# Five transposed weights for the backward pass: transposed by TensorE and kept in DRAM, or loaded by transposing DMAs

## The chip, the cores and the metric

The kernel runs on one core of a Trainium2 chip. The metric is the device time of one execution in microseconds (us). In the profile PE is TensorE (matmuls; PEld are its weight loads), DVE is VectorE, ACT is ScalarE, POOL is GpSimd and SP is the engine that issues all the DMAs of this kernel, on one queue.

## The reference

The reference computes a four-layer network and all its gradients. Layers 0 and 2 are the same linear-attention block, layers 1 and 3 the same gated block, each on a layernorm of the residual stream x, with shared weights:

```python
def _A_ref(x, wqkv, wo):          # H = 32 heads of 16
    q, k, v = (x @ wqkv) split into heads
    pq, pk = phi(q), phi(k)       # phi(t) = where(t > 0, t + 1, exp(t)) + 1e-6
    kv = einsum("bhsd,bhse->bhde", pk, v); z = einsum("bhsd->bhd", pk)
    o = einsum("bhqd,bhde->bhqe", pq, kv) / (einsum("bhqd,bhd->bhq", pq, z)[..., None] + 1e-6)
    return merge_heads(o) @ wo

def _B_ref(x, w_gate, w_up, w_down):
    h = sigmoid(x @ w_gate) * (x @ w_up)
    return h @ w_down

x = x + _A_ref(_layernorm(x), A_wqkv, A_wo)
x = x + _B_ref(_layernorm(x), B_w_gate, B_w_up, B_w_down)
...                                # the same two lines once more
_out, _vjp = jax.vjp(_f, A_x, A_wqkv, A_wo, B_w_gate, B_w_up, B_w_down)
return (_out, *_vjp(grad_out))
```

The sequence has 2048 rows (S), the width D is 512, the gated width F is 1376, everything in bfloat16. wqkv is 512 x 1536, wo 512 x 512, w_gate and w_up 512 x 1376, w_down 1376 x 512.

## The kernel before

The sequence is cut into 16 tiles of 128 rows (NST = 16, index `st`). The forward pass goes through the layers in order. `kq_fwd` makes an attention layer's k and q for all tiles; `ab_fwd` then goes once over the tiles and does, for each, the rest of the attention layer (`attn_y`, line 809 on TensorE) and the whole gated layer behind it (`gu`, line 864; `transposes`, line 878; `finish`, line 890). What the backward pass needs is stored in DRAM (tensors `sv_...`), since SBUF does not hold it.

The backward pass is `b_bwd_p1(3)`, the attention backward of layer 2 (`A2.first`, `A2.second`), `b_bwd_p1(1)`, and the attention backward of layer 0 (`A0.first`, `A0.second`). The weight gradients are sums over all tiles; generators (`p2_gen`, lines 1330 and 1342) hand out their matmuls in units, which are put between the matmuls of the attention passes, and what is left is done at the end. `p2_gen` loads one set of operands ahead (`p_set`).

The order of TensorE, DVE, ACT and POOL is the order in which the program states the work (`tc.manual_schedule(engines=EM)`) in most stages; in `second` and on SP's queue a scheduler places the instructions. Each engine takes its instructions in order, and SP issues DMAs in order; a DMA shares one of eight completion semaphores with the DMA eight places earlier and is issued once that one has landed.

The backward pass multiplies by transposed weights. They are made in the forward pass. A `Fill` object holds 16 groups for `ab_fwd` of layer 1 (`wT_groups_a`: wqkv and wo) and 34 groups for that of layer 3 (`wT_groups_b`: w_down, w_up, w_gate). A group is three or four 128 x 128 TensorE transposes into one PSUM tile `wT_ps` (lines 369, 395, 412) and one eviction on DVE or ACT (lines 341, 343). Six groups of each layer are put at the start of the stage (four in `A.tail`, one `A.extra`, one in tile 0); the others are spread over the later tiles:

```python
def share(self, st):
    return (self.n - self.done) // (NST - st)
```

In layer 1 this gives no group in tiles 1 to 5 and one in each tile from 6 on; in layer 3 one group in tiles 1 and 2, and two in each tile from 3 on. The groups of layer 1 are stored to DRAM (`wqkvT_d`, `woT_d`). Those of layer 3 are evicted right into `wdT`, `wuT` and `wgT`, where `b_bwd_p1(3)` uses them, and stored to DRAM too (`wdT_d`, `wuT_d`, `wgT_d`).

The backward weights live in a pool `wb` with three buffers: `w_c` (wdT, later MT and X of the attention), `w_a` (wuT, later wqkvT) and `w_b` (wgT, later woT and GT). So they are loaded anew for each layer: `load_a_weights` at the start of `A2.first` and `A0.first` (lines 247 to 252), `load_b_weights` ahead of `b_bwd_p1(1)` (lines 235 to 239). In `ABwd.first` the loads of the tiles' `pqn` (line 1463) and `phq_ld` (line 1031) stand behind them on SP's queue; DVE's step for a tile needs `phq_ld` (line 1453).

F is 10 chunks of 128 and one of 96 (`FLAST`). In `b_bwd_p1` the last chunk of `ddT` is transposed and multiplied with 96 rows, and evicted by a copy of its own (lines 1085 and 1087).

## Time and profile before

| what | value |
|---|---|
| time, median of 3 runs | 1215.07 us (1214.5 to 1217.31) |
| the profiled execution: time, span | 1216.08 us, 1214.3 us |
| granted TensorE clock, mean | 0.999 |
| PE busy | 1185.4 us, 98% of the span, 8646 matmuls |
| DVE, ACT, POOL busy | 726.9, 599.9, 259.1 us |
| DMA | 256.08 MB, 66.0% of 16 engines over the span |
| weight transposes on TensorE (`wT_ps`) | 196, in layer 1 from 72.6 to 214.0 us, in layer 3 from 277.6 to 428.0 us |
| plain reload of wdT, wuT, wgT (layer 1) | 1376, 1408, 1408 KB; 10.3, 6.5, 7.7 us to landing |
| plain loads of wqkvT and woT (layers 2 and 0) | 1536 and 512 KB; 9.0 and 8.2 us to landing, median of 2 |

The span is from the first to the last instruction; the execution's time has some us around it. [...] "Idle before, releaser" names what an engine waited for just before an instruction. The stages lie in the trace like this: layer 0's k and q to 72 us, layer 1's `ab_fwd` to 225, layer 2's k and q to 277, layer 3's `ab_fwd` to 433, `b_bwd_p1(3)` to 570, the attention backward of layer 2 to 707, held-back weight-gradient matmuls and `b_bwd_p1(1)` to 931, the attention backward of layer 0 to 1070, and the last weight gradients.

### The profile page before, as it was taken

The numbers are of one execution on the slowest core, as the hardware profiler recorded it, in microseconds if no ns is written. First come the engines' busy times: TensorE is split into PE (matmuls) and PEld (weight loads), VectorE is DVE, ScalarE is ACT, GpSimd is POOL, SyncE is SP. The second block draws the span as 40 slices with busy tenths as digits, with TensorE's granted clock in tenths as the row PEclk, the third lists the DMA queues.
The fourth block names the chain that finished last, engine by engine and source line by source line (L and its number), as shares of the span: only waits on it lengthen the run. The fifth ranks groups of instructions, "written<-read, shape, count | busy, mean of one in ns | idle before, by whom it ended". The sixth has DMA issues, their size and how long they took to land. (4 is left out here: it accounts for less than half of the span.)

```text
span 1214.3 us, 22436 instructions
## 1 busy us (share of the span) xinstructions
PE 1185.4 (98%) x8646; PEld 716.8 (59%) x8646; DVE 726.9 (60%) x1410; ACT 599.9 (49%) x1105; POOL 259.1 (21%) x467
## 2 busy tenths in 40 slices
PE   7989999998999999999999999999999999999998
PEld 4445555454555555555665566765556755577777
DVE  6778887777777556565786730056666966742221
ACT  5677776647767644445537631145445527620001
POOL 4236675204665410000110010000100101100000
PEclk9999999999999999999999999999999999999999
DMA  7934545435546696967866469687667766569974
GB/s 231 311 118 144 197 157 181 172 122 176 185 150 231 232 279 184 312 187 236 229 188 203 147 222 322 206 281 218 213 194 246 206 219 180 170 172 351 293 234 135
DMA packets 266203, 256.08 MB, mean 211 GB/s; under 512 B 43248, under 2 KB 250992, under 8 KB 261232
## 3 DMA queue, kind: packets, MB, share of 16 engines
q1 hardware_dynamic: 266096, 254.65, 66.0%
q8 instruction: 67, 1.10, 0.4%
q14 instruction: 40, 0.33, 0.1%
HBM read 135.69 MB, written 118.92 MB: 210 GB/s over the span
## 5 line engine op out<-in xcount | busy, mean ns | idle before, releaser
L1342 PE MATMUL p_ps<-p_set,p_a 128*128 128x256 bf16 (+1 forms) x1792 | 186.8, 263 | 0.0
L1016 DVE TENSOR_TENSOR dd<-dhh_ps,ssd 128x512 bf16<-128x512 f32 x144 | 82.5, 629 | 149.0 <-PE dhh_ps L1008 142.1
L1342 PEld LDWEIGHTS <-p_a 128*128 128x128 bf16 x1792 | 160.3, 98 | 18.7
L1085 ACT COPY ddT<-T_ps 128x1024 bf16<-128x1024 bf16 (+1 forms) x96 | 82.9, 868 | 126.5 <-PE T_ps L1083 126.5
L870 POOL TENSOR_TENSOR ssd_t<-hh_t,oms 128x512 bf16<-128x512 bf16 (+1 forms) x96 | 101.6, 1064 | 53.6 <-ACT out_t L212 40.9
L1117 PEld LDWEIGHTS <-ddT 128*128 128x128 bf16 (+1 forms) x704 | 66.4, 98 | 68.6
L864 PEld LDWEIGHTS <-hT 128*128 128x128 bf16 x768 | 71.2, 98 | 57.8 <-DVE hT L341 1.5
L982 POOL TENSOR_SCALAR ab<-c 128x2 f32<-128x2 f32 x64 | 12.5, 196 | 433.2 <-DVE junk L979 416.4
L864 PE MATMUL g_ps<-wg,hT 128*128 128x512 bf16 (+1 forms) x384 | 90.0, 357 | 1.1 <-DVE hT L341 1.1
L1321 DVE TENSOR_TENSOR dw_stg<-p_ps,dw_stg 128x512 bf16<-128x512 f32 (+2 forms) x43 | 28.4, 659 | 103.3 <-PE p_ps L1342 80.8
L864 PE MATMUL u_ps<-wu,hT 128*128 128x512 bf16 (+1 forms) x384 | 90.0, 357 | 0.0
L869 DVE TENSOR_TENSOR hh_t<-u_ps,ssd_t 128x512 bf16<-128x512 f32 (+1 forms) x96 | 61.0, 636 | 46.9 <-PE u_ps L864 26.7
L1117 PE MATMUL dh_ps<-wgT,ddT 128*128 128x512 bf16 (+1 forms) x352 | 86.2, 379 | 0.0
L1008 PE MATMUL dhh_ps<-wdT,gT 128*128 128x512 bf16 x372 | 82.5, 357 | 0.5 <-DVE dd L1016 0.5
L890 PE MATMUL y_ps<-wd,hhT 128*128 128x512 bf16 (+1 forms) x352 | 81.3, 379 | 0.6 <-DVE x L892 0.6
L1117 PE MATMUL dh_ps<-wuT,ddT 128*128 128x512 bf16 (+1 forms) x352 | 81.3, 379 | 0.0
L1330 PE MATMUL p_ps<-p_a,p_set 128*128 128x512 bf16 (+1 forms) x352 | 80.4, 379 | 0.0
L866 ACT ACTIVATE ssd_t<-g_ps 128x512 bf16<-128x512 f32 (+1 forms) x96 | 53.2, 554 | 31.7 <-PE g_ps L864 31.4
L974 ACT ACTIVATE t_sb<-dh_ps,rstd_all 128x512 f32<-128x512 f32 x64 | 44.0, 688 | 36.6 <-issue 18.4
L979 DVE SCALAR_TENSOR_TENSOR junk<-t_sb,h_ld 128x512 bf16<-128x512 f32 x60 | 41.2, 687 | 34.8 <-ACT t_sb L974 34.8
L1323 ACT CAST dw_stg<-p_ps 128x512 bf16<-128x512 f32 (+2 forms) x43 | 24.2, 563 | 72.1 <-PE p_ps L1342 51.8
L1330 PEld LDWEIGHTS <-p_set 128*128 128x128 bf16 (+1 forms) x352 | 34.4, 100 | 35.5
(236 smaller groups left out, 2184.9 us busy)
## 6 DMA issues: line engine op xcount, KB each, us to landing
p_set<-sv_hdd SPq DMA_DIRECT2D x30, 1024.0 KB, 6.4
sv_ssd<-ssd_t SPq DMA_DIRECT2D x32, 688.0 KB, 3.5
ssd<-sv_ssd SPq DMA_DIRECT2D x24, 688.0 KB, 5.0
sv_hdd<-dd SPq DMA_DIRECT2D x48, 320.0 KB, 3.3
sv_hdd<-hh_t SPq DMA_DIRECT2D x32, 320.0 KB, 2.6
p_set<-sv_dqk SPq DMA_DIRECT2D x8, 1024.0 KB, 5.4
h_ld<-sv_h SPq DMA_DIRECT2D x30, 256.0 KB, 4.5
p_a<-sv_h SPq DMA_DIRECT2D x12, 512.0 KB, 6.5
```

Of the source, the lines that this page charges most:

```text
L864: nc.tensor.matmul(ps[:, 0:w], lhsT=hT[:, kc, :], rhs=w_sb[:, kc, c0:c0 + w], start=(kc == 0), stop=(kc == NDC - 1))
L866: nc.scalar.activation(ssd_t[:, 0, c0:c0 + w], g_ps[:, 0:w], ACT.Sigmoid)
L869: nc.vector.tensor_tensor(hh_t[:, c0:c0 + w], u_ps[:, 0:w], ssd_t[:, 0, c0:c0 + w], ALU.mult)
L870: nc.gpsimd.tensor_tensor(ssd_t[:, 1, c0:c0 + w], hh_t[:, c0:c0 + w], oms[:, 0:w], ALU.mult)
L890: nc.tensor.matmul(y_ps[:], lhsT=T["hhT"][0:r, fc, :], rhs=k.wd[0:r, fc, :], start=(fc == 0), stop=(fc == NFC - 1))
L974: k.nc.scalar.activation(self.t[:], dh_ps, ACT.Identity, scale=rstd_col, accum_out=self.c12[:, 0:1])
L1008: k.nc.tensor.matmul(ps[:, 0:w], lhsT=gT[:, jc, :], rhs=k.wdT[:, jc, c0:c0 + w], start=(jc == 0), stop=(jc == NDC - 1))
L1016: k.nc.vector.tensor_tensor(dd[:, a, c0:c0 + w], ps[:, 0:w], ssd[:, a, c0:c0 + w], ALU.mult)
L1085: nc.scalar.copy(ddT[:, :, fcs[0]:fcs[0] + nfull, :], tps[:, :, 0:nfull, :])
L1117: nc.tensor.matmul(T["dh"][:], lhsT=T["ddT"][0:r, a, fc, :], rhs=(k.wuT, k.wgT)[a][0:r, fc, :], start=(i == 0), stop=(i == 2 * NFC - 1))
L1330: nc.tensor.matmul(ps[0:r, :], lhsT=set_t[:, st, j * P:j * P + r], rhs=g_all[:, st, :], start=(st == 0), stop=(st == NST - 1))
L1342: nc.tensor.matmul(ps[:, icl * w:(icl + 1) * w], lhsT=h_all[:, st, ic * P:(ic + 1) * P], rhs=set_t[:, st, 0:w], start=(st == 0), stop=(st ...
```

## The change

The five weights are no longer transposed by TensorE. Each buffer of the backward weights is loaded by transposing DMAs (`dma_start_transpose`) straight from the kernel's inputs, at every place where it was made or reloaded. `wT_groups_a`, `wT_groups_b` and the DRAM tensors of the transposed weights are gone, and both `Fill` objects are empty. `load_b_weights` is now called for layer 3 too, from `out_cb` of tile 1. A transposing DMA of w_up and w_gate moves chunks of 128 columns, so the last chunk is loaded from columns 1248 to 1375: its first 32 rows repeat columns that chunk 9 has, and a POOL memset zeroes them after the load. `b_bwd_p1` therefore treats the last chunk as a full one: 128 rows in the transposes and matmuls, and one eviction instead of two.

```diff
+    def load_b_weights():
+        wb = k.wb
+        k.wdT = wb.tile([P, NDC, F], BF16, name="wdT", tag="w_c")
+        nc.sync.dma_start_transpose(out=k.wdT[:], in_=B_w_down)
+        k.wuT = wb.tile([P, NFC, D], BF16, name="wuT", tag="w_a")
+        k.wgT = wb.tile([P, NFC, D], BF16, name="wgT", tag="w_b")
+        for t_sb, w_d in ((k.wuT, B_w_up), (k.wgT, B_w_gate)):
+            nc.sync.dma_start_transpose(out=t_sb[:, 0:NFC - 1, :], in_=w_d[:, 0:(NFC - 1) * P])
+            nc.sync.dma_start_transpose(out=t_sb[:, NFC - 1:NFC, :], in_=w_d[:, F - P:F])
+            nc.gpsimd.memset(t_sb[0:P - FLAST, NFC - 1, :], 0.0)
...
-            with tc.tile_pool(name="wt_stage", bufs=2, reuse_waits="tile") as wt_stage:
-                fill = Fill(wT_groups_a(k, wt_stage))
-                A.tail(fill)
-                ab_fwd(k, A, lns[1], fill, nxt=lns[2])
+            fill = Fill([])
+            A.tail(fill)
+            ab_fwd(k, A, lns[1], fill, nxt=lns[2])
...
             def out_cb(st):
+                if st == 1:
+                    k.load_b_weights()
...
-            fill = Fill(wT_groups_b(k, wb))
+            fill = Fill([])
...
-        def load_b_weights():
-            k.wdT = wb.tile([P, NDC, F], BF16, name="wdT", tag="w_c")
-            nc.sync.dma_start(out=k.wdT[:], in_=k.wT["wdT"].rearrange("(c p) f -> p c f", p=P))
-            k.wuT = wb.tile([P, NFC, D], BF16, name="wuT", tag="w_a")
-            k.wgT = wb.tile([P, NFC, D], BF16, name="wgT", tag="w_b")
-            for t_sb, t_d in ((k.wuT, k.wT["wuT"]), (k.wgT, k.wT["wgT"])):
-                nc.sync.dma_start(out=t_sb[:], in_=t_d.rearrange("(c p) j -> p c j", p=P))
...
-            nc.sync.dma_start(out=k.wqkvT[:], in_=k.wT["wqkvT"].rearrange("(c p) j -> p c j", p=P))
+            nc.sync.dma_start_transpose(out=k.wqkvT[:], in_=A_wqkv)
...
-            nc.sync.dma_start(out=k.woT, in_=k.wT["woT"].rearrange("(c p) j -> p c j", p=P))
+            nc.sync.dma_start_transpose(out=k.woT, in_=A_wo)
...
-                    r = fc_rows(fc)
-                    nc.tensor.transpose(tps[0:r, a, i, :], dd[:, a, fc * P:fc * P + r], k.ident[:])
-            if nfull > 0:
-                nc.scalar.copy(ddT[:, :, fcs[0]:fcs[0] + nfull, :], tps[:, :, 0:nfull, :])
-            if nfull < len(fcs):
-                nc.scalar.copy(ddT[0:FLAST, :, NFC - 1, :], tps[0:FLAST, :, nfull, :])
+                    c0 = min(fc * P, F - P)
+                    nc.tensor.transpose(tps[:, a, i, :], dd[:, a, c0:c0 + P], k.ident[:])
+            nc.scalar.copy(ddT[:, :, fcs[0]:fcs[0] + len(fcs), :], tps[:, :, 0:len(fcs), :])
...
-                r = fc_rows(fc)
-                nc.tensor.matmul(T["dh"][:], lhsT=T["ddT"][0:r, a, fc, :], rhs=(k.wuT, k.wgT)[a][0:r, fc, :],
+                nc.tensor.matmul(T["dh"][:], lhsT=T["ddT"][:, a, fc, :], rhs=(k.wuT, k.wgT)[a][:, fc, :],
```

On SP's queue the scheduler puts wdT's transposing DMA of layer 3 behind the last store of pk of layer 2, wuT's first one behind the store of X, and the other three behind the store of MT; they come ahead of the stores of layer 3's first tile. In `A2.first` the order on the queue stays: wqkvT, woT, three loads of pqn, then phq. In `A0.first` the first load of phq, which stood ahead of the three loads of pqn, now stands behind them. On POOL the two memsets of layer 3 stand together, behind the layernorm scalars of tile 3.

More of the change, by code (lines that the diff above doesn't have):

```diff
@@ L120 @@
         k.sv[l] = d
-    k.wT = dict(
-        wqkvT=dram.tile([3 * D, D], BF16, name="wqkvT_d"),
-        woT=dram.tile([D, D], BF16, name="woT_d"),
-        wgT=dram.tile([NFC * P, D], BF16, name="wgT_d"),
-        wuT=dram.tile([NFC * P, D], BF16, name="wuT_d"),
-        wdT=dram.tile([D, F], BF16, name="wdT_d"),
-    )
     k.dwp = dict(
@@ L133 @@
     )
+    def load_b_weights():
[8 more added lines that the diff above has]
+            nc.gpsimd.memset(t_sb[0:P - FLAST, NFC - 1, :], 0.0)
+    k.load_b_weights = load_b_weights
     k.rstd = [keep.tile([P, NST], F32, name=f"rstd_all{l}") for l in range(4)]
@@ L194 @@
             hctx.close()
-            wb = bctx.enter_context(tc.tile_pool(name="wbwd", bufs=1, side="right", reuse_waits="tile"))
+            wb = k.wb = bctx.enter_context(tc.tile_pool(name="wbwd", bufs=1, side="right", reuse_waits="tile"))
             ocur = {}
@@ L248, in load_a_weights @@
             k.wqkvT = wb.tile([P, 3 * NDC, D], BF16, name="wqkvT", tag="w_a")
-            nc.sync.dma_start(out=k.wqkvT[:], in_=k.wT["wqkvT"].rearrange("(c p) j -> p c j", p=P))
+            nc.sync.dma_start_transpose(out=k.wqkvT[:], in_=A_wqkv)
             woT_GT = wb.tile([P, 2, NDC, D], BF16, name="woT_GT", tag="w_b")
             k.woT, k.GT = woT_GT[:, 0, :, :], woT_GT[:, 1, :, :]
-            nc.sync.dma_start(out=k.woT, in_=k.wT["woT"].rearrange("(c p) j -> p c j", p=P))
-        k.load_b_weights, k.load_a_weights, k.load_MT = load_b_weights, load_a_weights, load_MT
+            nc.sync.dma_start_transpose(out=k.woT, in_=A_wo)
+        k.load_a_weights, k.load_MT = load_a_weights, load_MT
         R = P2Res(k,
@@ L353, in dram_batch @@
     return ap2d[batch_rows(b, nb), :].rearrange("(n p) d -> p n d", p=P)
-def wT_groups_a(k, stage):
-    nc = k.nc
-    groups = []
-    for w_sb, wT_d, C in ((k.wqkv, k.wT["wqkvT"], 3 * D), (k.wo, k.wT["woT"], D)):
-        for cc0 in range(0, C // P, 4):
-            holder = {}
-            for j in range(4):
-                def g(bank, w_sb=w_sb, wT_d=wT_d, cc0=cc0, j=j, holder=holder):
-                    if j == 0:
-                        holder["t"] = stage.tile([P, 4, D], BF16, name="wt_st")
-                    cc = cc0 + j
-                    ps = ps_tile(k, bank, [P, 8, P], BF16, "wT_ps")
-                    for rc in range(NDC):
-                        nc.tensor.transpose(ps[:, rc, :], w_sb[:, rc, cc * P:(cc + 1) * P], k.ident[:])
-                    def ev(eng):
-                        evac_copy(k, holder["t"][:, j, :], ps[:, 0:NDC, :].rearrange("p a b -> p (a b)"), eng)
-                        if j == 3:
-                            nc.sync.dma_start(
-                                out=wT_d[cc0 * P:(cc0 + 4) * P, :].rearrange("(n p) d -> p n d", p=P),
-                                in_=holder["t"][:])
-                    return ev
-                groups.append(g)
-    return groups
@@ L382, in wT_groups_b @@
-def wT_groups_b(k, wb):
-    nc = k.nc
-    groups = []
-    k.wdT = wb.tile([P, NDC, F], BF16, name="wdT", tag="w_c")
-    k.wuT = wb.tile([P, NFC, D], BF16, name="wuT", tag="w_a")
-    k.wgT = wb.tile([P, NFC, D], BF16, name="wgT", tag="w_b")
-    for cc in range(NDC):
-        for fs in range(3):
-            def g(bank, cc=cc, fs=fs):
-                fcs = fchunks_of_slice(fs)
-                ps = ps_tile(k, bank, [P, 8, P], BF16, "wT_ps")
-                for i, fc in enumerate(fcs):
-                    r = fc_rows(fc)
-                    nc.tensor.transpose(ps[:, i, 0:r], k.wd[0:r, fc, cc * P:(cc + 1) * P], k.ident[0:r, 0:r])
-                c0, w = FSL[fs]
-                def ev(eng):
-                    evac_copy(k, k.wdT[:, cc, c0:c0 + w], ps[:].rearrange("p a b -> p (a b)")[:, 0:w], eng)
-                    if cc == NDC - 1 and fs == 2:
-                        nc.sync.dma_start(out=k.wT["wdT"].rearrange("(c p) f -> p c f", p=P), in_=k.wdT[:])
-                return ev
-            groups.append(g)
-    for w_sb, wT_sb, wT_d in ((k.wu, k.wuT, k.wT["wuT"]), (k.wg, k.wgT, k.wT["wgT"])):
-        for cc in range(NFC):
-            def g(bank, w_sb=w_sb, wT_sb=wT_sb, wT_d=wT_d, cc=cc):
-                r = fc_rows(cc)
-                if cc == 0:
-                    nc.gpsimd.memset(wT_sb[FLAST:P, NFC - 1, :], 0.0)
-                ps = ps_tile(k, bank, [P, 8, P], BF16, "wT_ps")
-                for rc in range(NDC):
-                    nc.tensor.transpose(ps[0:r, rc, :], w_sb[:, rc, cc * P:cc * P + r], k.ident[:])
-                def ev(eng):
-                    evac_copy(k, wT_sb[0:r, cc, :], ps[0:r, 0:NDC, :].rearrange("p a b -> p (a b)"), eng)
-                    if cc == NFC - 1:
-                        nc.sync.dma_start(out=wT_d.rearrange("(c p) j -> p c j", p=P), in_=wT_sb[:])
-                return ev
-            groups.append(g)
-    return groups
@@ L1077, in transposes @@
             fcs = fchunks_of_slice(fs)
-            nfull = len([fc for fc in fcs if fc_rows(fc) == P])
             tps = ps_tile(k, "t", [P, 2, 4, P], BF16, "T_ps")
@@ L1115, in dh_mm @@
                 a, fc = divmod(i, NFC)
-                r = fc_rows(fc)
-                nc.tensor.matmul(T["dh"][:], lhsT=T["ddT"][0:r, a, fc, :], rhs=(k.wuT, k.wgT)[a][0:r, fc, :],
+                nc.tensor.matmul(T["dh"][:], lhsT=T["ddT"][:, a, fc, :], rhs=(k.wuT, k.wgT)[a][:, fc, :],
                                  start=(i == 0), stop=(i == 2 * NFC - 1))
```

## The prediction

> **What bounds the kernel now.** I read the page first, then TensorE's waits, its timeline, the DMA share by stretches, and last DVE's, SP's and POOL's timelines where the loaded weights are used. The chain of waits reaches back only to 1067 us, where the edit no longer acts, so the stages decide. In fences with columns "start us, us", x4 counts instructions.

> ```profile
> PE 1185.4 (98%) x8646; PEld 716.8 (59%) x8646; DVE 726.9 (60%) x1410; ACT 599.9 (49%) x1105; POOL 259.1 (21%) x467
> ```

> TensorE is busy 98% of the span, and its named waits sum to 24 us, most at the starts of stages or in the two attention backward passes. So removed TensorE work counts, at its price in the row of instructions, not at its shown duration. That price is in TensorE's timeline of the first GLU forward (layer 1):

> ```profile
> 114.01 1.03 PE L809 MATMUL y_ps<-M_sb,pqnT 128*128 128x512 bf16 x4
> ...
> 123.25 1.03 PE L809 MATMUL y_ps<-M_sb,pqnT 128*128 128x512 bf16 x4
> ...
> 132.23 1.03 PE L809 MATMUL y_ps<-M_sb,pqnT 128*128 128x512 bf16 x4
> 133.09 0.39 PE L369 MATMUL wT_ps<-ident,wqkv 128*128 128x128 bf16 x4
> 133.31 1.03 PE L864 MATMUL g_ps<-wg,hT 128*128 128x512 bf16 x4
> ...
> 141.45 1.03 PE L809 MATMUL y_ps<-M_sb,pqnT 128*128 128x512 bf16 x4
> ...
> 150.66 1.03 PE L809 MATMUL y_ps<-M_sb,pqnT 128*128 128x512 bf16 x4
> ```

> A group of four weight transposes moves the next matmul by 133.31 - 133.09 = 0.22 us (busy time says 0.39). L809 comes once per row tile: with a group the period is 9.21 to 9.22 us, without one 9.24 and 8.98 in turn, mean 9.11. So removing a group in layer 1 is worth 0.11, not 0.22: without it every second tile waits for DVE's pqnstage. The same in layer 3, with one and with two groups per tile:

> ```profile
> 291.80 1.03 PE L809 MATMUL y_ps<-M_sb,pqnT 128*128 128x512 bf16 x4
> ...
> 300.97 1.03 PE L809 MATMUL y_ps<-M_sb,pqnT 128*128 128x512 bf16 x4
> ...
> 338.42 1.03 PE L809 MATMUL y_ps<-M_sb,pqnT 128*128 128x512 bf16 x4
> ...
> 347.82 1.03 PE L809 MATMUL y_ps<-M_sb,pqnT 128*128 128x512 bf16 x4
> ```

> 9.17 with one group, 9.40 with two: here the second costs its full 0.23.

> **What goes.** 196 transposes in 50 groups. In each layer six groups stand at the start of the stage; behind them TensorE waits for hstage, hT or pqnstage anyway (0.95, 0.56 and 1.8 us in layer 1; 0.72, 0.58 and 1.88 in layer 3), and those chains run through DVE, POOL and ACT: worth 0. Ten groups in layer 1 at 0.11: 1.2 us. 28 in layer 3 at 0.22: 6.2 us, or 4 if the alternate wait of layer 1 shows up there (no tile in layer 3 is free of groups, so this is not seen; DVE has two instructions fewer per tile there, so I take 6.2). Sum **-7.4 us**, between -5 and -8.4 (38 groups at 0.22). The evictions (35 on DVE near 0.39, 15 on ACT near 0.59) and 6.4 MB of stores lie beside TensorE work: 0 by themselves. In the gate backward two ACT copies (579 and 375 ns) become one over 128x768, 32 times; no TensorE wait there names ddT, so 0; transposes and matmuls of 96 rows become 128, and rows show both forms at 218 to 219 and 379 to 381 ns: 0.

> **What comes: 14 transposing DMAs** on SP's queue, of which before has no row. The built program gives each a block of 16 source rows by 128 columns: pieces of 256 bytes at the source, 32 bytes per partition at the destination. The trace's packet records give 256-byte packets at 18 ns on each of 16 engines, 227 GB/s; 1024-byte packets, which the plain reloads use, at 49.6 ns, 330 GB/s; 4-byte packets take 9 ns and 192-byte ones 15, so 32-byte pieces near 10 ns would make 51 GB/s. The bounds are 51 and 330; I take 227, the row with the source's piece. [...]

> The three GLU weights are 4.29 MB (18.9 us at 227, about 12.7 plain), the two attention weights 2.10 MB (9.2 against 6.3).

> *Layer 3's load.* SP now carries wdT at about 264 us, wuT from 273, the rest after the store of MT at 279. Between 264 and 314 the DMA share is 0.45, so 22 + 19 = 41 of 50 us: hidden. A new wait comes with it: two POOL memsets of the padding rows must follow the landed transfers, and stand in POOL's order between these two:

> ```profile
> 313.91 0.26 POOL L433 TENSOR_SCALAR ln_nmr<-ln_mv,rstd_all 128x1 f32<-128x1 f32 x1
> 314.13 1.16 POOL L870 TENSOR_TENSOR ssd_t<-hh_t,oms 128x512 bf16<-128x512 bf16 x1
> ```

> Queued behind are ssd_t, prod and the layernorm scalars, for which every tile waits. At 227 the last transfer lands near 290, 24 us early: 1 us of POOL work, 0 on the path.

> *Layer 1's reload* (706 to 778 us, 60 of 72 us DMA-busy) grows by 6.2 us: 66 of 72, hidden behind the weight-gradient matmuls that fill TensorE there. SP's other loads there (p_set) queue behind; TensorE is 20.00 of 20 in these stretches, so small delays are covered.

> *Attention backward, layer 2.* Here nothing covers:

> ```profile
> 566.00:585.00 19.00, 19.00 (x108) 9.63 (x106) 7.46 (x16) 8.98 (x18) 1.75 (x4) 1.00 1.08 345
> ```

> ```profile
> 584.16 0.69 DVE L1453 SCALAR_TENSOR_TENSOR phq_ld<-phq_ld,rden_all 128x512 bf16<-128x512 bf16 x1 [8.63 <-DMA phq_ld<-sv_phq]
> ```

> The DMA engines are full (1.08, 345 GB/s), and DVE waits 8.63 us for phq_ld, which stands on the queue behind wqkvT, woT and three pqn loads. DVE then runs without a gap, 3.07 us per tile to 620, and TensorE already waits (1.04, 0.16, 0.26, 1.09 us). So 2.9 us more of transfer is **+2.9 us** (0 to 35).

> *Attention backward, layer 0.* DVE waits only 1.73 us there (phq at 938.46). In the new order of SP the first phq load also stands behind the three pqn loads (1.5 MB, 4.8 us), so it lands 2.9 + 4.8 = 7.7 us later. TensorE takes 3.37 us per tile against DVE's 3.07, and DVE may fall four dp buffers behind; stepping both forward gives TensorE 1.7 us of stall, of which 0.86 replaces one seen at 975.64: **+1.0 us** (0 to 33).

> Sum: -7.4 + 2.9 + 1.0 = -3.5 us. The profiled execution took 1216.08 us (span 1214.3), 1.0 above the median of 1215.07, so 1212.6 for such a run, and **1212 us** against the median. About 0.2%, 2.4 us, is what a measurement of this kernel can tell from no change.

> **Rivals.** *The transposing transfer is slower than 130 GB/s, and time ends slower.* For: the 32-byte pieces at the destination, and a stage at 345 GB/s that has nothing to give. Against: the source pieces match a row of 227. Layer 3 is covered while 4.29 MB land between 264 and 298, before the stores of its first tile are waited for by tile 2 (hh_t and ssd_t have two buffers): 126 GB/s. At 100 GB/s: layer 3 +9, layer 2's attention 21.0 - 6.3 = +15, layer 0's +13, the reload 60 - 12.7 + 43 = 90 in 72, +18; less 7.4: about **1262 us**. At 130: 1233. At 85, with the memset on POOL waiting past 314: 1286. At 51: about 1380. The two attention terms alone turn the sign at about 190 GB/s.

> *Blocks of 128x128 go one after another.* The smallest plain transfer of that size (32 KB, dw_stg) lands in 2.0 us; 131 and 64 blocks at 2.0 us are 262 and 128 us per set, some 700 us in all: **1900 us**. Nothing in the trace speaks for it but that row. [...]

> *The transfer keeps 330 GB/s.* Layer 2 then costs 0, and layer 0's 4.8 us stay inside its slack: 1215.07 - 7.4, about **1208 us**.

> **Chances.** Forecast (190 to 300 GB/s) 0.48, its own range 1207 to 1218, split 0.28 faster, 0.14 within 0.2% (if layer 3 gives 4 us instead of 6.2, or layer 0 costs 3), 0.06 slower. Transfers at 330 or more: 0.08, faster. Slow transfers (under 190): 0.38, slower. One after another: 0.06, slower. Together 0.36 faster, 0.14 same, 0.50 slower: the likeliest single case is slightly faster, but the sign is open. The range runs from 1206 to 1286; it leaves out rates under 85 GB/s (about 0.12), the serial case and little below.

> **What would show it.** Right: no wT_ps; L809's period in layer 3 near 8.95 and in layer 1 near 9.11; transposing DMAs of 1.4 MB landing in 7 to 9 us; DVE's first phq wait near 11.5 us at 575 and 9 at 937; POOL's memsets with no wait. Wrong: these DMAs landing in over 12 us; POOL's memset waiting on a DMA with ssd_t late behind it; TensorE waiting for p_set or wdT near 730 to 780; hh_t waiting for a store near 300; or SP held for many microseconds by one transposing issue (the plain one of wqkvT holds it 1.00 us).

## The result and the profile after

The changed kernel takes 1220.63 us (median of 20 runs, 1214.51 to 1224.92) against 1214.96 us (20 runs, 1212.16 to 1218.52): ratio 1.0040, 95% interval 1.0027 to 1.0054. It is slower by 0.4%, about twice what can be told from no change, where the forecast was slightly faster (1212).

The profile seems to say the opposite. Its span is 1212.8 us, less than the 1214.3 us before, because the profiled execution took 1214.51 us, the shortest of the twenty. The granted clock of each run explains the spread: it lies between 0.987 and 0.996, and the longer runs mostly have the lower one. So I split every time in two: the shortfall, span x (1 - granted clock), which is the time that TensorE's clock did not deliver, and the rest. (Some of the shortfall falls on moments when TensorE is idle anyway, so it is an upper bound of the loss: over 32 runs of the changed kernel the time grows 0.77 us with each us of it. The clock is on record to three digits, so one step of it is 1.2 us of shortfall.)

| kernel | time, median | shortfall, median | rest, median |
|---|---|---|---|
| before (83 runs beside the experiments) | 1215.1 | 1.2 | 1213.4 |
| after (32 runs) | 1220.6 | 9.8 | 1209.5 |

The rest became 3.9 us shorter, where the forecast was 3.5. But the shortfall is an upper bound of the loss, and so 3.9 is one of the gain. A line through the 32 runs of after meets zero shortfall at 1212.2 us (give or take 1.3), one through the 83 of before at 1213.4: by that the gain at full clock is 1.2 us. So most of the miss of 8.6 us, an estimated 6.6 (0.77 x the 8.6 us of added shortfall), is in a term that the forecast does not have: the clock. The other 2 us are in terms of the sum that came out smaller or larger than forecast.

The lines of after that answer to those of before. The first, from the page: TensorE's work fell by 8.4 us.

```profile
PE 1177.0 (97%) x8450; PEld 706.2 (58%) x8450; DVE 717.3 (59%) x1375; ACT 591.5 (49%) x1058; POOL 260.1 (21%) x469
```

TensorE's timeline, row L739 (L809 before), in layer 1 and then in layer 3:

```profile
112.10 1.03 PE L739 MATMUL y_ps<-M_sb,pqnT 128*128 128x512 bf16 x4
121.37 1.03 PE L739 MATMUL y_ps<-M_sb,pqnT 128*128 128x512 bf16 x4
130.32 1.03 PE L739 MATMUL y_ps<-M_sb,pqnT 128*128 128x512 bf16 x4
...
335.34 1.03 PE L739 MATMUL y_ps<-M_sb,pqnT 128*128 128x512 bf16 x4
344.29 1.03 PE L739 MATMUL y_ps<-M_sb,pqnT 128*128 128x512 bf16 x4
```

The period is 9.27 and 8.95 in turn in layer 1 (mean 9.11) and 8.95 in layer 3: both as forecast. The attention backward of layer 2, first the stretch, then DVE's timeline, then TensorE's, after and then before (the stretch: its length, the busy time of PE, PEld, DVE, ACT and POOL with their instructions, then granted clock, DMA share, GB/s):

```profile
559.00:578.00 19.00, 18.26 (x103) 9.13 (x101) 5.75 (x11) 8.31 (x16) 1.56 (x3) 1.00 1.08 288
```

```profile
579.26 0.69 DVE L1378 SCALAR_TENSOR_TENSOR phq_ld<-phq_ld,rden_all 128x512 bf16<-128x512 bf16 x1 [11.83 <-DMA phq_ld<-sv_phq]
```

```profile
581.50 1.89 PE L1319 MATMUL dp_ps<-MT_X,gT 128*128 128x512 bf16 x4 [4.24 <-ACT gT L1312]
583.18 0.63 PE L1311 MATMUL gT_ps<-ident,g 128*128 128x128 bf16 x4
```

```profile
586.40 1.04 PE L1394 MATMUL dp_ps<-MT_X,gT 128*128 128x512 bf16 x4 [1.04 <-ACT gT L1387]
587.28 0.39 PE L1386 MATMUL gT_ps<-ident,g 128*128 128x128 bf16 x4
```

DVE waits 11.83 us for phq (8.63 before; 11.5 forecast), and TensorE 4.24 us (1.04 before). But look at the durations: the four matmuls of L1319 take 1.89 us where they took 1.04, those of L1311 0.63 where they took 0.39. TensorE is at half clock. Four stretches of after show where that begins (columns as above):

```profile
77.90:81.30 3.40, 1.37 (x14) 0.89 (x13) 3.03 (x8) 2.20 (x4) 2.75 (x5) 1.00 0.13 40
81.30:84.70 3.40, 3.40 (x14) 1.47 (x12) 0.00 (x0) 2.05 (x6) 1.59 (x2) 0.50 0.79 299
576.20:579.60 3.40, 1.06 (x5) 0.37 (x3) 0.34 (x1) 0.00 (x0) 0.00 (x0) 1.00 1.06 360
579.60:586.40 6.80, 4.90 (x25) 3.06 (x26) 6.66 (x14) 3.66 (x7) 1.18 (x2) 0.50 1.01 277
```

In 77.90 to 81.30 TensorE is busy 1.37 of 3.40 us, at full clock; in the next 3.4 us it is fully busy and gets half the clock. The same at 576, twice as long. The first place is the start of layer 1, where the forecast gave the removed transposes a value of 0. TensorE's waits there (its timeline, rows with a wait), before and then after:

```profile
74.92 0.40 PE L334 MATMUL ln_tp<-ident,hstage 128*128 128x128 bf16 x4 [0.95 <-ACT hstage L438]
76.11 1.04 PE L864 MATMUL g_ps<-wg,hT 128*128 128x512 bf16 x4 [0.56 <-DVE hT L341]
84.72 0.40 PE L334 MATMUL ln_tp<-ident,pqnstage 128*128 128x128 bf16 x4 [1.80 <-DVE pqnstage L788]
```

```profile
71.33 0.40 PE L331 MATMUL ln_tp<-ident,hstage 128*128 128x128 bf16 x4 [2.18 <-ACT hstage L368]
72.52 1.04 PE L794 MATMUL g_ps<-wg,hT 128*128 128x512 bf16 x4 [0.79 <-DVE hT L338]
81.13 0.50 PE L331 MATMUL ln_tp<-ident,pqnstage 128*128 128x128 bf16 x4 [2.03 <-DVE pqnstage L718]
```

The same instructions wait for the same tiles; the waits are longer by 1.23, 0.23 and 0.23 us, about what the 16, 4 and 4 transposes in front of them had filled. The half clock that follows costs 1.7 us: the start of L739 at 76.43 us is 3.59 us earlier than that of L809 in before, the next one, at 84.93, only 1.91.

POOL's memsets, between the two instructions that the forecast named, start without a wait:

```profile
310.49 0.27 POOL L363 TENSOR_SCALAR ln_nmr<-ln_mv,rstd_all 128x1 f32<-128x1 f32 x1
310.69 0.52 POOL L136 MEMSET wuT<- 32x512 bf16 x1
311.15 0.51 POOL L136 MEMSET wgT<- 32x512 bf16 x1
311.64 1.96 POOL L800 TENSOR_TENSOR ssd_t<-hh_t,oms 128x512 bf16<-128x512 bf16 x2
```

### The profile page after: what moved, and what is told of

Same layout as the page of the kernel before. It is cut to its first block, busy times and chain, and to the rows that moved or that the text cites. A ratio compares the mean times of both kernels' runs of the same rounds, so it can differ in the third digit from the quotient of the medians.

```text
span 1212.8 us, 21930 instructions
## 1 busy us (share of the span) xinstructions
PE 1177.0 (97%) x8450; PEld 706.2 (58%) x8450; DVE 717.3 (59%) x1375; ACT 591.5 (49%) x1058; POOL 260.1 (21%) x469
## 3 DMA queue, kind: packets, MB, share of 16 engines
q8 instruction: 66, 1.08, 0.4%
## 5 line engine op out<-in xcount | busy, mean ns | idle before, releaser
L1013 ACT COPY ddT<-T_ps 128x1024 bf16<-128x1024 bf16 (+1 forms) x96 | 89.7, 939 | 127.4 <-PE T_ps L1012 127.4
L1042 PEld LDWEIGHTS <-ddT 128*128 128x128 bf16 x704 | 66.3, 98 | 68.7 <-ACT ddT L1013 0.5
L1042 PE MATMUL dh_ps<-wgT,ddT 128*128 128x512 bf16 x352 | 86.1, 379 | 0.0
L1042 PE MATMUL dh_ps<-wuT,ddT 128*128 128x512 bf16 x352 | 81.2, 379 | 0.0
```

Of the source, the lines that this page charges most:

```text
L1013: nc.scalar.copy(ddT[:, :, fcs[0]:fcs[0] + len(fcs), :], tps[:, :, 0:len(fcs), :])
L1042: nc.tensor.matmul(T["dh"][:], lhsT=T["ddT"][:, a, fc, :], rhs=(k.wuT, k.wgT)[a][:, fc, :], start=(i == 0), stop=(i == 2 * NFC - 1))
```

## The experiments

Each kernel was timed beside the kernel before. The expectations speak of theory S (the stall in the attention backward and the half clock behind it) against T (the transposing transfers cost wherever they run), and then of theory C (the removed transposes had kept the clock up) against P (the half-clock stretches come otherwise).

**r1_again**: the changed kernel, unchanged.

> The changed kernel once more, for a second profile and the clock of every run. In its first profile the span is 1212.8 us, shorter than the 1214.3 us of the kernel before, while its median time is 5.7 us longer; the granted clock was 0.995 there and 0.987 to 0.996 over its 20 runs, and time falls with the clock. Theory S (stall and clock): TensorE stalls 4.24 us at 577 us for the late phq load, and the clock then runs at half for two stretches of 3.41 us; in other executions more such stretches occur. Then this profile, if its time is near the median of 1220.6 us, shows five or more half-clock stretches, most of them between 570 and 590 us. Theory T (transfers): the transposing loads cost the time wherever they run, in layer 3 and in the reload too; then a slower execution shows longer waits there at full clock.

1220.15 us, ratio 1.0039 (1.0024 to 1.0055), shortfall 10.4. The profiled execution was again a short one (span 1215.4 us), so the five stretches that were expected were not seen: it has two half-clock stretches of 3.41 us (at 15.6 and 83.9 us) and one of 6.83 us (at 582.2), the last behind a stall of 4.89 us. New to both theories is the stretch at 84, where there is no transfer to wait for.

**r2_glu_only**: wdT, wuT and wgT by transposing DMAs, wqkvT and woT as before.

```diff
-            fill = Fill([])
...
+            with tc.tile_pool(name="wt_stage", bufs=2, reuse_waits="tile") as wt_stage:
+                fill = Fill(wT_groups_a(k, wt_stage))
...
-            nc.sync.dma_start_transpose(out=k.wqkvT[:], in_=A_wqkv)
+            nc.sync.dma_start(out=k.wqkvT[:], in_=k.wT["wqkvT"].rearrange("(c p) j -> p c j", p=P))
...
```

> Only wdT, wuT and wgT come by transposing DMAs; wqkvT and woT are made by TensorE in layer 1 and stored and loaded as before. Theory S: the attention stages are as before, so only the gain of layer 3 is left, 28 groups at 0.22 us: 1215 - 6 = 1209 us, ratio 0.995, and a clock of 0.998 or more. Theory T: 4.29 MB of the 6.4 MB per load round are still transposed, so most of the loss stays: ratio 1.002 to 1.004.

1212.38 us, ratio 0.9974 (0.9959 to 0.9988), shortfall 4.2, rest 1207.3. Faster, so T falls. But the clock is not that of before: its profile has half-clock stretches at 278.7 and 288.9 us, the start of layer 3, where the transposes are gone, and none at the start of layer 1, where they are still there. A third, at 582.5 us, goes with a TensorE wait of 2.33 us in the attention backward, though the loads there are plain ones.

**r3_att_only**: only wqkvT and woT by transposing DMAs, the rest as before.

```diff
-                fill = Fill(wT_groups_a(k, wt_stage))
...
+            fill = Fill([])
...
-            nc.sync.dma_start(out=k.wqkvT[:], in_=k.wT["wqkvT"].rearrange("(c p) j -> p c j", p=P))
+            nc.sync.dma_start_transpose(out=k.wqkvT[:], in_=A_wqkv)
...
```

> Only wqkvT and woT come by transposing DMAs, everything else is as before. Theory S: the gain of layer 1 (1.2 us) and the whole stall of the attention backward of layer 2, 3.2 us more waiting and some 3.4 us of half clock or more: 1215 - 1.2 + 6.6 = 1220 us, ratio 1.004 to 1.008, clock 0.990 to 0.996. Theory T: a third of the transposed bytes, ratio 0.999 to 1.002.

1219.96 us, ratio 1.0040 (1.0026 to 1.0053), shortfall 6.1, rest 1213.2: as S expected. The stall at 580 us is 4.71 us, with 6.83 us of half clock. The shortfalls of r2 and r3 above that of before (3.0 and 4.9) add up to nearly that of after (8.6). The rests do not: -6.1 and -0.2 against -3.9. That difference was not followed up.

**r4_att_late**: the changed kernel with the two attention loads moved behind tile 8.

```diff
-            k.wqkvT = wb.tile([P, 3 * NDC, D], BF16, name="wqkvT", tag="w_a")
-            nc.sync.dma_start_transpose(out=k.wqkvT[:], in_=A_wqkv)
...
+        def load_a_weights_T():
             k.wqkvT = wb.tile([P, 3 * NDC, D], BF16, name="wqkvT", tag="w_a")
+            nc.gpsimd.memset(k.wqkvT[:, 0, 0:1], 0.0)
+            nc.gpsimd.memset(k.woT[:, 0, 0:1], 0.0)
             nc.sync.dma_start_transpose(out=k.wqkvT[:], in_=A_wqkv)
             nc.sync.dma_start_transpose(out=k.woT, in_=A_wo)
...
+                if st == 8:
+                    k.load_a_weights_T()
```

> The changed kernel, with the two transposing loads of wqkvT and woT put behind tile 8 of the first attention backward pass, so that the phq and pqn loads are no longer behind them (a POOL memset of one column of each buffer holds them back). Theory S: the stall at 577 us and its half clock are gone, so the forecast gain of 7.4 us shows: 1207 to 1209 us, ratio 0.994. If SP held for 6 to 9 us in the middle of the pass delays a later phq load, a new stall of 1 to 4 us shows near tile 12, and the ratio is 0.996 to 1.000. Theory T: the transfers cost the same elsewhere, ratio 1.002 to 1.005.

1210.10 us, ratio 0.9959 (0.9941 to 0.9977), shortfall 4.8, rest 1204.2. The direction is as S expected, with no new stall, and the rest is 9.2 us below that of before, more than the 7.4 expected. The run moved more than the two loads: on SP's queue the first loads of phq (569.94 us) now also stand ahead of those of pqn (571.38 us), and TensorE's waits from 560 to 640 us, 2.6 us in before, are down to 0.5 us. But 1 to 3 us of the expected gain are missing, and they are in the shortfall: the profile has 23.9 us of half clock, at 15.6, 73.6, 87.3, 281.8 and 295.5 us, 20.5 of them at the starts of layers 1 and 3. With the stall removed, those starts were what was left, and theory C was formed.

**r5_late_fill**: r4 and six groups of four idle transposes where the weight transposes had stood.

```diff
+def fill_groups(k, n=6, m=4):
+    def g(bank):
+        ps = ps_tile(k, bank, [P, 8, P], BF16, "fill_ps")
+        for rc in range(m):
+            k.nc.tensor.transpose(ps[:, rc, :], k.ident[:], k.ident[:])
+        return lambda eng: None
+    return [g] * n
...
-            fill = Fill([])
+            fill = Fill(fill_groups(k))
```

> The kernel with the late attention loads (r4_att_late), and six groups of four idle transposes (of the identity, never read) at the starts of layers 1 and 3, where the six groups of weight transposes stood before the change. In r4_att_late half-clock stretches lie between 73 and 91 us and between 281 and 299 us, the starts of these two layers; time x (1 - clock) comes to 4.8 us there, 9.8 us in the changed kernel, 1.2 us in the kernel before, and the time less this loss is 1204.2, 1209.6 and 1213.4 us. Theory C (clock): the transposes had filled TensorE's waits there and so kept the clock up. Then the loss falls to 1 to 2 us and the time to 1205 to 1206 us, ratio 0.992. Theory P (phase): the stretches come from somewhere else or by chance. Then the clock stays at 0.996 and the time at 1210 us or above it, ratio 0.996.

1205.98 us, ratio 0.9924 (0.9906 to 0.9942), shortfall 2.4, rest 1203.2: theory C. Work that nobody reads makes the kernel faster. The stretches at both starts (columns as above), r4 first and r5 second:

```profile
69.00:96.00 27.00, 22.00 (x125) 10.98 (x124) 17.20 (x36) 15.82 (x30) 12.06 (x19) 0.81 0.23 81
275.00:302.00 27.00, 21.97 (x120) 10.49 (x118) 16.61 (x35) 16.11 (x31) 9.95 (x17) 0.81 1.01 246
```

```profile
69.00:96.00 27.00, 23.40 (x163) 13.05 (x161) 19.37 (x40) 17.05 (x35) 12.91 (x22) 0.94 0.37 129
275.00:302.00 27.00, 23.40 (x171) 13.20 (x170) 19.84 (x41) 18.50 (x37) 14.89 (x22) 1.00 1.06 225
```

PEclk rises from 0.81 to 0.94 and 1.00, and in the same 27 us TensorE gets through 38 and 51 more instructions, of which the idle transposes are 24. TensorE's waits at layer 1's start are 1.22, 0.57 and 1.81 us, near those of before.

**r6_after_fill**: the changed kernel with the same filler, its loads where they were.

> The changed kernel with the same six groups of idle transposes at the starts of layers 1 and 3, and its attention loads where they are. Theory C: of the 9.8 us lost to the clock the part at these starts goes, about 4 us, and that of the stall at 577 us stays, about 5 us: 1215 to 1216 us, ratio 1.000 to 1.001. Theory P: 1220 us, ratio 1.004.

1218.61 us, ratio 1.0039 (1.0024 to 1.0055), shortfall 7.3, rest 1211.3. Neither number was expected: the shortfall fell by 2.5 us, but the rest rose by 1.8. The stall at 579 us is 5.54 us.

**r7_before_moved**: the kernel before, with the six start groups of layers 1 and 3 given to later tiles (`skip` begins at 6).

```diff
     def mm(self, bank):
+        if self.skip > 0:
+            self.skip -= 1
+            return lambda eng: None
...
-        return (self.n - self.done) // (NST - st)
+        return (self.n - self.done) // (NST - st) if st > 0 else 0
```

> The kernel before, with the six groups of weight transposes at the starts of layers 1 and 3 moved into the later tiles of the same layer: the same work on every engine, and the starts empty. The prediction gave the six groups at each start a value of 0. Theory C: the starts now lose clock, 3 to 4 us, and the six groups cost 0.11 to 0.22 us each in the later tiles, 2 us: 1219 to 1221 us, ratio 1.004, clock 0.995 to 0.997. Theory P: only the 2 us, 1217 us, ratio 1.0015, clock 0.999.

1227.00 us, ratio 1.0094 (1.0075 to 1.0113), shortfall 7.4, rest 1219.0. The starts lose clock as C expected (half-clock stretches at 74.0, 84.3 and 292.5 us). The rest is 3 to 4 us longer than expected. Two side effects are seen: the evictions now reach into the last tiles (TensorE's transposes wait 2.0 us in all for wgT's evictions after 400 us), and a wait of 1.44 us for dd in `b_bwd_p1(3)` grew to 1.75 us, at 515 us, with one more half-clock stretch at 517.7. So this run shows the sign, not the size.

**r8_att_plain**: the changed kernel, the two attention loads as plain DMAs, so that the two weights arrive untransposed.

```diff
-            nc.sync.dma_start_transpose(out=k.wqkvT[:], in_=A_wqkv)
+            nc.sync.dma_start(out=k.wqkvT[:].rearrange("p (c t) j -> p c t j", t=3), in_=A_wqkv.rearrange("(c p) (t j) -> p c t j", p=P, t=3))
...
```

> The changed kernel with the two loads of wqkvT and woT as plain DMAs of as many bytes from the same inputs, at the same places of SP's queue: wqkv and wo arrive untransposed, so the gradients are not the reference's. If the transposing transfer itself makes the stall at 577 us (its issue holds SP 8.8 us where the plain one held it 1.0 us, and it moves about 290 GB/s), the stall falls from 4.2 to 4.9 us to 1 to 2.5 us, the half clock behind it mostly goes, and the time is 1211 to 1214 us, ratio 0.998. If the order of the queue makes it (phq behind three pqn loads), the stall stays at 4 us or more and the time at 1219 to 1221 us, ratio 1.004.

1213.82 us, ratio 0.9994 (0.9977 to 1.0010), rest 1206.8; the stall is 1.53 us. So the transposing transfer itself makes the greater part of the stall: with plain loads it is 1.04, 2.33 and 1.53 us (before, r2, r8), with transposing ones at this place of the queue 4.24 to 5.61 us (after, r1, r3, r6, r12). SP's timeline (start, time on the queue), after and then r8:

```profile
559.23 8.82 SPq L246 DMA_TRANSPOSE wqkvT<-in_A_wqkv_dram  x1
568.15 2.12 SPq L249 DMA_TRANSPOSE woT_GT<-in_A_wo_dram  x1
570.37 1.62 SPq L1388 DMA_DIRECT2D pqn<-sv_pqn  x3
572.08 1.99 SPq L961 DMA_DIRECT2D phq_ld<-sv_phq  x2
```

```profile
559.39 0.43 SPq L246 DMA_DIRECT2D wqkvT<-in_A_wqkv_dram  x1
561.36 0.37 SPq L249 DMA_DIRECT2D woT_GT<-in_A_wo_dram  x1
561.85 5.13 SPq L1388 DMA_DIRECT2D pqn<-sv_pqn  x3
567.07 3.80 SPq L961 DMA_DIRECT2D phq_ld<-sv_phq  x3
```

From wqkvT's issue to phq's it takes 12.85 us with transposing loads and 7.68 us with plain ones. The shortfall stays at 6.7 us, with hardly a stall left to make it. (In layer 0 the first phq load stands ahead of pqn again in this kernel, so r8 says nothing of the term there.)

**r9_late_fill8**: r5 with `m=8`.

> The kernel of r5_late_fill with eight idle transposes in each of the twelve start groups instead of four. r5_late_fill took 1206.0 us, 2.4 us of it lost to the clock, and its profile still has one half-clock stretch at 74 us, behind gaps of 1.22 us; without any filler the gaps there are 2.17 us. Theory C: twice the filler closes more of the gaps, the loss falls to 1.2 us, that of the kernel before, and the time is 1204 to 1205 us, ratio 0.991, if the longer filler (0.44 us a group) still fits into the waits. If it does not fit, the time less the loss rises by 1 to 3 us and the total is 1206 to 1208 us. Theory P: clock and time as without filler, 1210 us.

1207.33 us, ratio 0.9938 (0.9920 to 0.9956), shortfall 2.4, rest 1205.4. By the medians more filler saves no more clock, and the rest is 2 us longer, as was expected for a filler that does not fit into the waits; but the interval overlaps that of r5.

**r10_late_2, r11_late_fill_2, r12_after_fill_2**: r4, r5 and r6 again, on one chip.

> The kernel of r4_att_late (late attention loads, no filler) again, on the same chip as the next two, so that filler and no filler are compared directly: r4 and r5 ran on different occasions and their intervals, 0.9941 to 0.9977 and 0.9906 to 0.9942, touch. Theory C: loss to the clock 4 to 6 us, time 1209 to 1210 us. Theory P: no difference from the next kernel.

> The kernel of r5_late_fill (late loads and four idle transposes in each of the twelve start groups) beside r10_late_2. Theory C: loss 1 to 2.5 us, 3 to 4 us faster than r10_late_2, 1205 to 1206 us. Theory P: the same as r10_late_2 within 1 us.

> The kernel of r6_after_fill (the changed kernel with the filler, loads where they are) beside the other two. r6 gave 1218.6 us, with the loss down from 9.8 to 7.3 us and the time less the loss up from 1209.6 to 1211.3 us; its profile had a longer stall at 579 us, 5.54 instead of 4.24 to 4.89 us. Theory C with a stall that varies: loss 5 to 7 us, time less loss 1209 to 1211 us, 1215 to 1218 us in all. If the filler lengthens the stall itself, the profile again shows 5.4 us or more there, and the time less the loss is 1211 us or more.

1209.72, 1206.70 and 1219.12 us; ratios 0.9944 (0.9926 to 0.9963), 0.9917 (0.9900 to 0.9935) and 1.0032 (1.0016 to 1.0048); shortfalls 4.8, 2.4 and 7.3. The filler is worth 3.0 us beside the late loads (r4 to r5, on two chips: 4.1). Without them no gain can be told (ratios 1.0039 and 1.0032 against 1.0040 for after): the stall at 579 us is 5.61 us again, the wait at 946 us 2.59 us (1.41 in after) with a half-clock stretch at 947.9 us, and the rest is 1212.2 us. So in both of its profiles the kernel with the filler has a longer stall. SP issues the same DMAs in the same order, but wqkvT holds it 10.07 us instead of 8.82. Within that transfer lies a stretch in which the DMA engines are shown as full and move little (r12, columns as above):

```profile
566.00:568.00 2.00, 2.00 (x14) 1.05 (x13) 1.74 (x3) 1.59 (x3) 0.05 (x1) 1.00 1.24 78
568.00:570.00 2.00, 2.00 (x14) 1.01 (x12) 0.72 (x2) 1.41 (x3) 0.59 (x1) 1.00 1.28 290
```

The trace has one thing that goes with the pause. A packet of 16 KB on the queue for instructions (q8) starts at 565.38 us and takes 1.53 us; behind it some twenty 256-byte packets of the load, which take 18 ns elsewhere, take 1.3 to 1.5 us. In r6 it is the same, with the 16 KB packet at 565.86 us and 82 GB/s from 566 to 568 us. In after and r1 no such packet falls into this transfer, and none of its 256-byte packets takes over 0.54 us. That the one makes the other is not shown by an experiment.

## Why the prediction was wrong

The step that failed is the price of a TensorE wait. The prediction counted a wait by its length alone: what stood in a wait that is there anyway was worth nothing, and a longer wait cost its added length. The runs show a second price: half the clock for 3.41 us or more behind a stretch in which the waits left TensorE little to do (in after 1.38 us of work in the 3.41 us from 77.87 us, and 1.7 us lost behind it).

Term by term, against the lag of the changed kernel behind the kernel before in the two profiles (the start of each L739 and each dp_ps matmul; negative is earlier; both profiles have one half-clock stretch before 100 us):

- *Layer 1, ten groups, -1.2 us.* Right: the lag goes from -1.9 to -3.0 us, the period is 9.11.
- *Layer 3, 28 groups, -6.2 us.* Too large by 1.1 us: -3.0 at its start, -8.1 us at 569. The period is 8.95, so the alternate wait of layer 1 does not appear; but one tile takes 10.73 us instead of 9.33 in before, since TensorE now waits 1.61 us for pqnstage at 313.7.
- *Rate of the transposing transfer, 227 GB/s.* Its packets are 256 bytes at 18 ns, the row that was taken; alone on the queue it moves 290 GB/s, since the packets' times overlap (DMA share 1.28, as in the line of r12 from 568 us). wdT lands in 8.3 us in layer 3 and 13.1 us in the reload, wqkvT in 11.1 and 8.8 us. No rival on the rate came true, although SP was held for many microseconds by one issue, which the prediction had put among the signs of being wrong.
- *Layer 3's load and layer 1's reload, 0.* Right. Of the reload, 706 to 778 us, 0.99 is DMA time (0.83 before), and POOL's memset waits 24.7 us for wgT, a sign that the prediction had also named; but TensorE's waits in 700 to 800 us are 1.6 us against 1.0 (1.06 of them for p_set, named as a sign too).
- *Attention backward of layer 2, +2.9 us.* The waits are near the forecast (DVE 11.83 for 11.5; TensorE +3.2). From wqkvT's issue to DVE's step with phq it takes 20.0 us, 17.1 in before and 17.1 in r8: 3.0 us more, near the 2.9 forecast. That is in part luck, since the reason given was the rate: at the 290 GB/s seen, 2.10 MB would take an estimated 0.9 us more than plain, not 2.9. What the other 2 us are, SP held or the moments of low rate at the transfer's end (171 and 187 GB/s from 569.2 to 571.2 us), was not separated. What failed is what follows from a TensorE wait of 4 us: 6.83 us of half clock. The lag goes from -8.1 to -4.9 us with the wait and to -2.7 us with the half clock, then back to -3.9 us by 613 us, since a wait that TensorE had there in before (1.09 us) is gone: +4.2 in all.
- *Attention backward of layer 0, +1.0 us.* DVE waits 9.08 us (9 forecast), TensorE 1.41 and 0.86: the 0.86 that the new stall was to replace stayed. The lag goes from -3.4 to -1.6 us, +1.8.
- *The six groups at each start, 0.* The same step failed here. In waiting time it is right: the chains through hstage, hT and pqnstage are no longer than before. In clock it is wrong: with the transposes TensorE was busy 1.79 us of the 3.41 us that hold most of the wait for pqnstage (before, 81.12 us), and the granted clock stayed at 1.00; without them 1.38 us (after, 77.87 us), and it fell to 0.50.

What stands ahead of a half-clock stretch can be counted in the 14 profiles. In after the record of the granted clock has 0.50 for 3.413 us from 81.28 us and for 6.827 us from 579.62 us, in before for 3.413 us from 16.27 us, and 1.00 everywhere else from 6.2 us to the last cells of the kernel. Within one profile the stretches begin whole multiples of 3.413 us apart: 498.34 us in after, 146 of them; 58.0, 13.7, 194.5 and 13.7 us in r4, 17, 4, 57 and 4. So I laid a grid of 3.413 us over each profile, in phase with its own half-clock stretches, and took TensorE's busy share in every grid cell at full clock, from 8 us on and without the last cells of the kernel. Of the 31 cells behind which the clock fell to 0.50, 27 were busy 41% or less; the other four lay between 43 and 49%. No cell of 41% or less stayed without consequence, and none over 49% had one. In after the cells ahead of the two stretches were busy 1.38 and 1.10 us of 3.41 (40% at 77.87 us, 32% at 576.16), in before 1.02 us (30% at 12.86); the least busy cells with full clock behind them were at 1.53, 1.54 and 1.64 us (45, 45 and 48%; after, 67.63, 275.82 and 9.61 us). Behind a cell at half clock the shares are about twice those: seven such cells, busy up to 79%, were followed by another at half clock (in after the one at 579.58 us, 1.49 us busy, 44%), the other 31, busy 83% or more, by full clock (in before the one at 16.27 us, 3.18 us, 93%). That is how the waits of 4 us, and in r4 two waits close together (2.17 and 0.79 us), came to 6.83 us.

A wait of 2.03 us that falls wholly into one cell leaves 1.38 of 3.41 us, 40%: half clock, at 81.28 us of after. A wait of 1.81 us leaves an estimated 1.60 us, 47%, between the 41 and the 49%, where some cells had half clock behind them and others, such as the three of 45 to 48% in after, had none. At layer 1's start the longest waits of r4 are 2.17 and 2.04 us, at a clock of 0.81 from 69 to 96 us; those of r5, with the idle transposes, are 1.22 and 1.81 us, at 0.94. The cells do not lie alike in the two profiles of the changed kernel: the stretch at 81.28 us of after begins 23 cells and 2.8 us from the start of the span, that at 83.9 us of r1 24 cells and 2.0 us. And the same wait can cost 1.7 us (half of 3.41) or nothing: in after's own profile the 2.03 us in layer 1 were followed by half clock, 2.03 us at the same place of layer 3 (286.7 us) fell into two cells, busy 2.01 and 2.78 us of 3.41 (59 and 81%), and were not. By that I explain the spread of after, 1214.5 to 1224.9 us, and why its own profile showed so little of the loss; that one and r1's are of runs of 1214.51 and 1217.09 us, so neither shows a long run.

What is shown: the attention loads (r3, r8, r4) and the empty starts (r4 against r5, and again r10 against r11) each cost time. What is argued: how the 8.6 us of extra shortfall divide between them. Moving the attention loads takes 5.0 us off it (after to r4), the filler 2.4 or 2.5 (r4 to r5, after to r6); r8 puts both starts at up to 5.5 us, r3 the stall with layer 1's start at up to 4.9.

The transposing DMAs with late attention loads and idle transposes at two starts (r5, r11) make the kernel 0.8% faster than the kernel before, the best version of this study.

## What to carry to other kernels

Removing TensorE work that sits in TensorE's waits was not free here: where a cell of 3.41 us was left busy 41% or less, half clock followed, at a cost of 1.7 us in after at 81.28 us, and behind four cells of 43 to 49% too. So ask what busy share each such stretch keeps without the work, and let a run show what a low one costs. Read the granted clock of all runs before the profile: the one profile of after was its shortest run (1214.51 us, clock 0.995, where the median is 1220.63). A transposing load moved nearly as much per second here (290 GB/s, against 345 in the same stage of before) but held the issuing queue for most of its run (8.82 of 11.1 us), so put the small loads that someone waits for ahead of it, as r4 did.
